# The last row of the last weight: loaded, multiplied, added and stored in two halves

## The chip, the cores and the metric

One core of a Trainium2 chip. The metric is device time in microseconds (us) of that core; lower is better. The **time** is the metric. The **span** is what the profile covers, from the first to the last recorded instruction. Each run reports both, the span to 0.1 us. Time minus span is called **the time outside the span**.

In the lines of the profile, PE is TensorE, which multiplies (PEld is its loading of weights), DVE is VectorE, ACT is ScalarE, POOL is GpSimd and SP is the sync engine; a q after the name marks the engine's sequencer, which also issues the transfers (DMA), so "the ACT queue" is ACT issuing a transfer. SBUF is the core's working memory, PSUM the memory, in banks, in which TensorE sums. A load has **landed** when the last of its writes to a semaphore, the counter that engines wait on, is recorded. The **tail** is what lies between the last landing of w4 and the end of the span.

## The reference, cut to what matters

The kernel decodes one token: an attention block over a cache of 65536 keys and values (4 heads of 128, bf16) and, in parallel, a small MLP; both outputs are added to the residual.

```
A = attention(xn, k_cache, v_cache, wq) @ wo            # o (4096) @ wo (4096 x 1024)
B = x1 + gelu(layernorm(x1) @ w3) @ w4                  # gh (3584) @ w4 (3584 x 1024)
out = x + A + B                                         # 1024 numbers, bf16
```

Everything that is read once per call comes from HBM, 170 MB, and w4 comes last.

## The kernel before: the parts the change touches

w4 is kept as 128 partitions by 28 rows of 1024 columns: row r on partition p is weight row 28p + r. It arrives in four loads; the last brings row 27 alone. One bank of PSUM collects the 1024 outputs as four strips of 256 columns, in partitions 0, 32, 64 and 96, which four column groups of TensorE fill side by side: the last row's four matmuls start within 10 ns of each other and take 270 ns each.

```python
w4_parts = [(0, 17), (17, 7), (24, 3), (27, 1)]          # (first row, rows): one load each, sync queue
OUT = S_ps[:, 0, 0:256]                                  # PSUM bank 0

def out_rows(items, reads, last=False):
    fns = []
    for lhs, rhs in items:                               # gh column r (128x1), w4 row r (128x1024)
        for jj in range(4):
            fns.append(lambda e, lhs=lhs, rhs=rhs, jj=jj: e.matmul(
                S_ps[32 * jj:32 * jj + 1, 0, 0:256], lhs, rhs[:, 256 * jj:256 * jj + 256],
                start=False, stop=last, tile_position=(0, 32 * jj), skip_group_check=True))
    _grp(q_pe, fns, reads=reads, writes=[b_OUT], partial=True)
...
resid_rows()          # residual into bank 1
wo_rows()             # attention output @ wo into bank 1, then moved to bank 0
for i, (r0, nr) in enumerate(w4_parts):
    out_rows([(gh_bf[:, r:r + 1], KV[:, 2, r * D:(r + 1) * D]) for r in range(r0, r0 + nr)],
             [b_W4[i], b_gh], last=(i == len(w4_parts) - 1))
_op(q_dve, lambda e: e.tensor_copy(orow[:, :], OUT), ...)                 # cast to bf16
ev_out = _dma(q_sp, chan("out"), lambda e: e.dma_start(out=..., in_=orow[0:97:32, :]), ...)
q_sp.wait_all([ev_out])
```

## Time and profile before

| | before |
|---|---|
| time, median | 400.6 us (400.57 to 400.77, 3 runs) |
| span of the profiled run | 399.08 us |
| bytes read | 169.87 MB, 426 GB/s over the span |
| last landing of w4 to the end of the span | 2.52 us |

The kernel is a stream of loads with a short tail: the packets of the loads fill 98.7% of the 16 DMA engines' span, and what the engines compute is hidden under the loads, except for what must follow the last landing. The prediction below shows the lines. Two more from the page's DMA part: the number of DMA packets, and the packets that carry instructions rather than data.

```profile
DMA packets 3759, 169.97 MB, mean 426 GB/s; under 512 B 548, under 2 KB 552, under 8 KB 808
...
q8 instruction: 5, 0.08, 0.1%
```

### The profile page before, as it was taken

To read this page: it belongs to the slowest core of one execution; us is meant where nothing else is said; L and a number is where in the kernel's file an instruction comes from. 1 tells how busy PE (TensorE), PEld (TensorE's weight loads), DVE (VectorE), ACT (ScalarE), POOL (GpSimd) and SP (SyncE) were. 2 spreads that over 40 slices of the span, in tenths; PEclk is the share of its full clock that TensorE was granted. 3 is DMA by queue.
4 is the path that set the end of the run, shared out by engine and by line. 5 is a ranking of instruction groups with operands and counts; after the bars stand their busy time and mean duration, and the time that the engine had idled before them with its cause. 6 is when DMAs were issued, how large, how long until landed. Compare 5 with 4: busy or idle time off the path is not lost.

```text
span 399.1 us, 3429 instructions
## 1 busy us (share of the span) xinstructions
PE 168.9 (42%) x1523; PEld 59.0 (15%) x1484; DVE 221.4 (55%) x260; ACT 23.9 (6%) x50; POOL 7.7 (2%) x31
## 2 busy tenths in 40 slices
PE   0034767338033713460357036413541362137394
PEld 0011334012001210110012001101120110012232
DVE  0024222994298549833984597269647952895201
ACT  1000000011001100110011002000100110011000
POOL 5000000000000000000000000000000000000000
PEclk9998568555655665575557555855585558555969
DMA  9999899999999999999999999999999999999995
GB/s 420 420 388 493 383 441 466 447 415 427 420 427 429 434 460 434 434 427 420 434 427 420 466 440 434 421 420 434 427 427 466 434 440 420 420 427 434 418 414 229
DMA packets 3759, 169.97 MB, mean 426 GB/s; under 512 B 548, under 2 KB 552, under 8 KB 808
## 3 DMA queue, kind: packets, MB, share of 16 engines
q1 hardware_dynamic: 3608, 169.87, 98.7%
q8 instruction: 5, 0.08, 0.1%
q10 hardware_dynamic: 144, 0.00, 0.0%
q14 instruction: 2, 0.02, 0.0%
HBM read 169.87 MB, written 0.00 MB: 426 GB/s over the span
## 4 chain that ended last, share of the span: by engine, by line
DMA 59%; DVE 25%; PE 12%; issue 1%; ACT 1%; SPq 1%; POOL 0%
DMA KV<-in_A_k_cache_dram 45%; DVE KV L460 18%; DMA KV<-in_B_w_dram 8%; DMA KV<-in_A_x_dram 6%; PE S_ps L411 3%; PE OT_ps L518 2%; DVE mrow L481 2%; PE M_ps L426 2%; PE S_ps L474 2%; PE S_ps L379 1%; ACT p_sb L496 1%; DVE Yall L395 1%; DVE pT_f L509 1%; DVE pT_f L419 1%; PE PT_ps L505 0%
## 5 line engine op out<-in xcount | busy, mean ns | idle before, releaser
L460 DVE STREAM_TRANSPOSE KV<-KV 128x4096 f32<-128x4096 f32 x32 | 140.3, 4422 | 44.3 <-DMA KV<-in_A_k_cache_dram 44.3
L474 PE MATMUL S_ps<-KV,Ycur 128*32 128x512 bf16 x512 | 60.7, 624 | 132.5 <-DVE KV L460 132.5
L518 PE MATMUL OT_ps<-KV,pT_f 128*32 128x512 bf16 x512 | 47.2, 511 | 4.0 <-issue 3.0
L474 PEld LDWEIGHTS S_ps<-KV,Ycur 128*32 128x32 bf16 x512 | 14.3, 126 | 160.0 <-DVE KV L460 142.4
L496 ACT ACTIVATE p_sb<-S_ps,brun 128x1024 bf16<-128x1024 f32 x16 | 17.8, 1114 | 276.6 <-DVE brun L494 176.1
L509 DVE STREAM_TRANSPOSE pT_f<-PT_ps 128x512 f32<-128x512 f32 x32 | 22.5, 702 | 14.0 <-PE PT_ps L505 14.0
L481 DVE TENSOR_REDUCE mrow<-S_ps 128x1 f32<-128x1024 f32 x16 | 19.3, 1205 | 11.3 <-PE S_ps L474 11.3
L484 PE MATMUL M_ps<-Rm,Lmat 128*128 128x16 bf16 x16 | 3.1, 194 | 38.0 <-DVE Rm L482 38.0
L529 DVE SCALAR_TENSOR_TENSOR O_acc<-O_acc,ff,OT_ps 128x512 f32<-128x512 f32 x12 | 9.0, 748 | 14.7 <-PE OT_ps L518 14.7
L518 PEld LDWEIGHTS OT_ps<-KV,pT_f 128*32 128x32 bf16 x512 | 13.1, 115 | 23.8 <-issue 16.4
L411 PE MATMUL S_ps<-KV 128*32 128x512 bf16 x88 | 12.1, 538 | 2.7 <-DVE KV L359 2.7
L339 DVE CAST KV<-KV 128x8 f32<-128x8 bf16 x1 | 0.2, 172 | 22.2 <-DMA KV<-in_A_x_dram 22.2
L578 PE MATMUL S_ps<-KV,o_bf 128*1 128x512 bf16 x64 | 9.9, 484 | 4.5 <-DMA KV<-in_A_wo_dram 4.5
L505 PE MATMUL PT_ps<-p_sb,permR 128*128 128x512 bf16 x16 | 9.7, 607 | 0.8
L426 PE MATMUL M_ps<-ident_f,pT_f 64*128 64x2 f32 (+2 forms) x32 | 7.9, 373 | 2.5 <-DVE pT_f L419 2.5
L484 PEld LDWEIGHTS M_ps<-Rm,Lmat 128*128 128x128 bf16 x16 | 1.7, 104 | 49.3 <-DVE Rm L482 49.3
L582 DVE COPY pT_f<-S_ps 1x512 f32<-1x512 f32 x1 | 0.7, 679 | 14.4 <-PE S_ps L578 14.4
L426 PEld LDWEIGHTS M_ps<-ident_f,pT_f 64*128 64x128 f32 (+2 forms) x32 | 7.7, 326 | 4.7 <-DVE pT_f L419 3.1
L419 DVE COPY pT_f<-S_ps 64x512 f32<-64x512 f32 (+1 forms) x3 | 2.1, 685 | 10.8 <-PE S_ps L411 10.8
L505 PEld LDWEIGHTS PT_ps<-p_sb,permR 128*128 128x128 bf16 x32 | 3.3, 102 | 27.5 <-ACT p_sb L496 14.7
L364 PE MATMUL M_ps<-KV 8*128 8x8 bf16 x1 | 0.2, 184 | 16.1 <-DVE Dmat_f L363 16.1
L642 POOL MEMSET pT_f<- 64x512 f32 x1 | 0.5, 520 | 312.4 <-PE OT_ps L518 312.4
(88 smaller groups left out, 90.2 us busy)
## 6 DMA issues: line engine op xcount, KB each, us to landing
KV<-in_B_w_dram SPq DMA_DIRECT2D x1, 7168.0 KB, 48.0
KV<-in_B_w_dram SPq DMA_DIRECT2D x1, 4352.0 KB, 27.4
KV<-in_B_w_dram SPq DMA_DIRECT2D x2, 2048.0 KB, 28.3
KV<-in_B_w_dram SPq DMA_DIRECT2D x1, 1792.0 KB, 31.3
KV<-in_B_w_dram SPq DMA_DIRECT2D x1, 768.0 KB, 32.7
KV<-in_B_w_dram SPq DMA_DIRECT2D x1, 256.0 KB, 32.9
KV<-in_A_k_cache_dram SPq DMA_DIRECT2D x8, 46.7
KV<-in_A_v_cache_dram SPq DMA_DIRECT2D x8, 28.1
```

The lines of the kernel that those rows point to most:

```text
L411: fns.append(lambda e, j=j, k=k, mv=mv: e.matmul(S_ps[32 * (k % 4):32 * (k % 4) + 32, bank + k // 4, :], vec[:, j:j + 1].broadcast_to([P, ...
L419: _op(q_dve, lambda e, b=b, nb=nb: e.tensor_copy(pT_f[0:32 * nb, b, :], S_ps[0:32 * nb, bank + b, :]), reads=[b_S[bank + b]], writes=[b_pT ...
L426: fns.append(lambda e, b=b, nb=nb, c=c: e.matmul(M_ps[:, c0 + 16 * b + c:c0 + 16 * b + 4 * nb:4], pT_f[0:32 * nb, b, c:512:4], ident_f[0:3 ...
L460: _op(q_dve, lambda e: e.transpose(out=KV32[:, s, o:o + 4096], in_=KV32[:, s, o:o + 4096]), reads=[b_KV[s][sub]], writes=[b_KV[s][sub]], l ...
L474: fns.append(lambda e, we=we, cm=cm, mv=mv: e.matmul(S_ps[32 * cm:32 * cm + 32, n % 4, :], Ycur[:, we, :, :].rearrange("p a g -> p (a g)") ...
L481: _op(q_dve, lambda e: e.reduce_max(mrow[:, k:k + 1], S_ps[:, 2 * k:2 * k + 2, :].rearrange("p b c -> p (b c)"), axis=AX.X), reads=b_S[2 * ...
L496: _op(q_act, lambda e: e.activation(p_sb[:, :, :].rearrange("p b c -> p (b c)"), S_ps[:, 2 * k:2 * k + 2, :].rearrange("p b c -> p (b c)") ...
L505: _op(q_pe, lambda e: e.matmul(PT_ps[:, :], permR[:, :], p_sb[:, n % 2, :], start=True, stop=True), reads=[b_p[n % 2], b_const], writes=[b ...
L509: _op(q_dve, lambda e: e.transpose(out=pT_f[:, n % 2, :], in_=PT_ps[:, :]), reads=[b_PT], writes=[b_pT[n % 2]], loop=True)
L518: fns.append(lambda e, q=q, q4=q4: e.matmul(OT_ps[32 * q4:32 * q4 + 32, g % 2, :], pT_bf[:, n % 2, q, :, 1], KV[:, s, 8192 * sub + 512 * q ...
L529: _op(q_dve, lambda e: e.scalar_tensor_tensor(out=O_acc[:, 0:512], in0=O_acc[:, 0:512], scalar=ff[:, k:k + 1], in1=OT_ps[:, k, :], op0=ALU ...
L578: _grp(q_pe, [lambda e, j=j, jj=jj: e.matmul(S_ps[32 * jj:32 * jj + 1, 1, :], o_bf[:, j:j + 1], KV[:, 0, j * D + 512 * jj:j * D + 512 * (j ...
```

## The change

The intent is a shorter tail. The last row arrives as two loads of 512 columns. Rows 0 to 23, the residual and wo are summed in bank 0 as before, but that sum is copied to SBUF ahead of time; rows 24 to 27 go into two other banks, one for each half of the columns. When a half has landed, its four matmuls have 128 columns, one add of 128 columns joins the bank with the copied sum and casts, and a store writes that half: the first from the ACT queue, the second from the sync queue. The second half's matmuls reuse the weights that the first half loaded. To make the halves contiguous, the columns of all strips are permuted (the residual and wo groups change addresses only). Cut to its core:

```diff
-w4_parts = [(0, 17), (17, 7), (24, 3), (27, 1)]
+w4_parts = [(0, 17 * D), (17 * D, 24 * D), (24 * D, 27 * D), (27 * D, 27 * D + 512), (27 * D + 512, 28 * D)]
...
+        def out_halves(r, halves, i, first=False, last=False):
+            def mm(e, hf, jj):
+                f = kept_matmul if halves == (1,) else ...          # ordinary matmul, fresh weights
+                return f(e, S_ps[32 * jj:32 * jj + 1, 2 + hf, 0:128], gh_bf[:, r:r + 1], w4_row(r, jj)[:, hf, :], (0, 32 * jj))
...
-        for i, (r0, nr) in enumerate(w4_parts):
-            out_rows(...)
-        _op(q_dve, lambda e: e.tensor_copy(orow[:, :], OUT), reads=[b_OUT], writes=[b_orow])
-        ev_out = _dma(q_sp, chan("out"), lambda e: e.dma_start(out=..., in_=orow[0:97:32, :]), reads=[b_orow])
-        q_sp.wait_all([ev_out])
+        for i in range(n_bulk):                                     # rows 0 to 23
+            out_rows(i)
+        _op(q_dve, lambda e: e.tensor_copy(ost, S_ps[:, 0, 0:256]), reads=[b_S[0]], writes=[b_ost])
+        for r in range(24, 27):
+            out_halves(r, (0, 1), 2, first=(r == 24))
+        ev_out = []
+        for hf, q_out in ((0, q_act), (1, q_sp)):
+            out_halves(27, (hf,), 3 + hf, last=True)
+            _op(q_dve, lambda e, hf=hf: e.tensor_tensor(out=orow[:, 128 * hf:128 * hf + 128],
+                in0=ost[:, 128 * hf:128 * hf + 128], in1=S_ps[:, 2 + hf, 0:128], op=ALU.add), ...)
+            ev_out.append(_dma(q_out, chan("out%d" % hf), lambda e, hf=hf: e.dma_start(out=..., in_=...), ...))
+        q_sp.wait_all(ev_out)
```

More of the change, by code (lines that the diff above doesn't have):

```diff
@@ L286, in bass_parallel_sum__gqa_block_cached__mixer_s_mlp__decode_kernel @@
         b_mrow = [_B(), _B()]; b_R = [_B(), _B()]; b_B = [_B(), _B()]; b_brun = [_B(), _B()]; b_dd = [_B(), _B()]; b_ff = [_B(), _B()]; b_lp = [_B(), _B()]
-        b_Oacc = _B(); b_L = _B(); b_cb = _B(); b_cbW = _B(); b_Mc = _B(); b_o = _B(); b_orow = _B()
+        b_Oacc = _B(); b_L = _B(); b_cb = _B(); b_cbW = _B(); b_Mc = _B(); b_o = _B(); b_orow = [_B(), _B()]
         def kv_load(s, ch, src, n, bufs=None):
@@ L550, in combine, with weights_of, keep_weights @@
             _op(q_dve, lambda e: e.tensor_copy(o_bf[32 * h:32 * h + 32, :], cb_o[0:32, :]), reads=[b_cb], writes=[b_o], partial=True)
-        w4_parts = [(0, 17), (17, 7), (24, 3), (27, 1)]
+        def weights_of(i):
+            return (i.tile_position, i.tile_size, str(i.ins[1].memref), i.ins[1].offset, str(i.ins[1].ap))
+        def keep_weights(i, name=""):
+            r = mybir.InstMatmult(name=name or i.name, engine=i.engine, ins=list(i.ins), outs=list(i.outs), debug=i.debug, start_tensor_calc=i.start_tensor_calc,
+                                  stop_tensor_calc=i.stop_tensor_calc, tile_size=i.tile_size, tile_position=i.tile_position,
+                                  bass_skip_group_check=i.bass_skip_group_check, ldweights=False)
+            return r
@@ new lines, in kept_matmul @@
+        def kept_matmul(e, out_, lhs, rhs, pos):
+            i = e.matmul(out_, lhs, rhs, start=False, stop=True, tile_position=pos, skip_group_check=True).ins
+            body = nc.m.functions[0].blocks[-1].instructions
+            at = max(k for k, j in enumerate(body) if j.name == i.name)
+            assert body[at].opcode == "Matmult" and any(j.opcode == "Matmult" and weights_of(j) == weights_of(i) for j in body[at - 6:at])
+            del body[at]
+            return e.add_instruction(keep_weights(i, "I-%d" % (1000000 + int(i.name[2:]))))
@@ L553, in bass_parallel_sum__gqa_block_cached__mixer_s_mlp__decode_kernel @@
+        w4_parts = [(0, 17 * D), (17 * D, 24 * D), (24 * D, 27 * D), (27 * D, 27 * D + 512), (27 * D + 512, 28 * D)]
         b_W4 = [_B() for _ in w4_parts]
         def w4_dma(i):
-            r0, nr = w4_parts[i]
-            _dma(q_sp, chan("w4%d" % i), lambda e: e.dma_start(out=KV[:, 2, r0 * D:(r0 + nr) * D], in_=rows_src(B_w4, r0, nr)), writes=[b_W4[i]])
-        OUT = S_ps[:, 0, 0:256]
-        b_OUT = b_S[0]
-        def out_rows(items, reads, last=False):
-            fns = []
-            for lhs, rhs in items:
-                for jj in range(4):
-                    fns.append(lambda e, lhs=lhs, rhs=rhs, jj=jj: e.matmul(
-                        S_ps[32 * jj:32 * jj + 1, 0, 0:256], lhs, rhs[:, 256 * jj:256 * jj + 256],
-                        start=False, stop=last, tile_position=(0, 32 * jj), skip_group_check=True))
-            _grp(q_pe, fns, reads=reads, writes=[b_OUT], partial=True)
+            c0, c1 = w4_parts[i]
+            _dma(q_sp, chan("w4%d" % i), lambda e: e.dma_start(out=KV[:, 2, c0:c1], in_=rows_src(B_w4, 0, KT_F)[:, c0:c1]), writes=[b_W4[i]])
@@ new lines, in bass_parallel_sum__gqa_block_cached__mixer_s_mlp__decode_kernel, with w4_row, out_rows @@
+        n_bulk = 2
+        b_half = [b_S[2], b_S[3]]
+        ost = pT_f[:, 1, 0:256]
+        b_ost = b_pT[1]
+        def w4_row(r, jj):
+            return KV[:, 2, r * D:(r + 1) * D].rearrange("p (h j n) -> p j h n", h=2, j=4)[:, jj, :, :]
+        def out_rows(i):
+            c0, c1 = w4_parts[i]
+            _grp(q_pe, [lambda e, r=r, jj=jj: e.matmul(
+                S_ps[32 * jj:32 * jj + 1, 0, 0:256].rearrange("p (h n) -> p h n", h=2), gh_bf[:, r:r + 1], w4_row(r, jj),
+                start=False, stop=(i == n_bulk - 1), tile_position=(0, 32 * jj), skip_group_check=True) for r in range(c0 // D, c1 // D) for jj in range(4)],
+                reads=[b_W4[i], b_gh], writes=[b_S[0]], partial=True)
@@ new lines, in out_halves @@
+        def out_halves(r, halves, i, first=False, last=False):
+            def mm(e, hf, jj):
+                f = kept_matmul if halves == (1,) else lambda e, *a: e.matmul(*a[:3], start=first, stop=last, tile_position=a[3], skip_group_check=True)
+                return f(e, S_ps[32 * jj:32 * jj + 1, 2 + hf, 0:128], gh_bf[:, r:r + 1], w4_row(r, jj)[:, hf, :], (0, 32 * jj))
+            _grp(q_pe, [lambda e, hf=hf, jj=jj: mm(e, hf, jj) for hf in halves for jj in range(4)],
+                 reads=[b_W4[i], b_gh], writes=[b_half[hf] for hf in halves], partial=not first)
@@ L571, in resid_rows @@
         def resid_rows():
+            idc = ident_f[:, :].rearrange("p (h j n) -> p j h n", h=2, j=2)
             _grp(q_pe, [lambda e, j=j, jj=jj: e.matmul(
-                S_ps[32 * jj:32 * jj + 1, 1, j:512:8], acc[:, j:j + 1], ident_f[:, 64 * jj:64 * jj + 64],
+                S_ps[32 * jj:32 * jj + 1, 1, :].rearrange("p (h n e) -> p h n e", h=2, e=8)[:, :, :, j], acc[:, j:j + 1], idc[:, jj, :, :],
                 start=(j == 0), stop=False, tile_position=(0, 32 * jj), skip_group_check=True) for j in range(KT_D) for jj in range(2)],
@@ L578, in wo_rows @@
             _grp(q_pe, [lambda e, j=j, jj=jj: e.matmul(
-                S_ps[32 * jj:32 * jj + 1, 1, :], o_bf[:, j:j + 1], KV[:, 0, j * D + 512 * jj:j * D + 512 * (jj + 1)],
+                S_ps[32 * jj:32 * jj + 1, 1, :].rearrange("p (h n) -> p h n", h=2), o_bf[:, j:j + 1],
+                KV[:, 0, j * D:(j + 1) * D].rearrange("p (h j n) -> p j h n", h=2, j=2)[:, jj, :, :],
                 start=False, stop=(j == 31), tile_position=(0, 32 * jj), skip_group_check=True) for j in range(32) for jj in range(2)],
@@ L583, in wo_rows @@
             _op(q_act, lambda e: e.activation(pT_f[32:33, 0, :], S_ps[32:33, 1, :], ACTF.Copy), reads=[b_S[1], b_pT[0]], writes=[b_pT[1]])
+            src = pT_f[0:64, 0, :].rearrange("p (h j n) -> p j h n", h=2, j=2)
             _grp(q_pe, [lambda e, jj=jj: e.matmul(
-                S_ps[32 * jj:32 * jj + 1, 0, 0:256], ident_f[0:64, 32 * (jj // 2):32 * (jj // 2) + 1], pT_f[0:64, 0, 256 * (jj % 2):256 * (jj % 2) + 256],
+                S_ps[32 * jj:32 * jj + 1, 0, 0:256].rearrange("p (h n) -> p h n", h=2), ident_f[0:64, 32 * (jj // 2):32 * (jj // 2) + 1], src[:, jj % 2, :, :],
                 start=True, stop=False, tile_position=(0, 32 * jj), skip_group_check=True) for jj in range(4)],
-                reads=[b_pT[0], b_pT[1], b_const], writes=[b_OUT])
+                reads=[b_pT[0], b_pT[1], b_const], writes=[b_S[0]])
         def loop_sync(h):
@@ L644, in bass_parallel_sum__gqa_block_cached__mixer_s_mlp__decode_kernel @@
         wo_rows()
-        for i, (r0, nr) in enumerate(w4_parts):
-            out_rows([(gh_bf[:, r:r + 1], KV[:, 2, r * D:(r + 1) * D]) for r in range(r0, r0 + nr)], [b_W4[i], b_gh], last=(i == len(w4_parts) - 1))
-        _op(q_dve, lambda e: e.tensor_copy(orow[:, :], OUT), reads=[b_OUT], writes=[b_orow])
-        ev_out = _dma(q_sp, chan("out"), lambda e: e.dma_start(out=out[0, 0, :].rearrange("(j n) -> j n", j=4), in_=orow[0:97:32, :]), reads=[b_orow])
-        q_sp.wait_all([ev_out])
+        for i in range(n_bulk):
[6 more added lines that the diff above has]
+            out_halves(27, (hf,), 3 + hf, last=True)
+            _op(q_dve, lambda e, hf=hf: e.tensor_tensor(out=orow[:, 128 * hf:128 * hf + 128], in0=ost[:, 128 * hf:128 * hf + 128], in1=S_ps[:, 2 + hf, 0:128], op=ALU.add),
+                reads=[b_ost, b_half[hf]], writes=[b_orow[hf]])
+            ev_out.append(_dma(q_out, chan("out%d" % hf), lambda e, hf=hf: e.dma_start(
+                out=out[0, 0, 512 * hf:512 * hf + 512].rearrange("(j n) -> j n", j=4), in_=orow[0:97:32, 128 * hf:128 * hf + 128]), reads=[b_orow[hf]]))
+        q_sp.wait_all(ev_out)
         code = nc.m.functions[0].blocks[0].instructions
@@ L706, in bass_parallel_sum__gqa_block_cached__mixer_s_mlp__decode_kernel @@
                 continue
-            key = (i.tile_position, i.tile_size, str(i.ins[1].memref), i.ins[1].offset, str(i.ins[1].ap))
+            key = weights_of(i)
             if key == prev and i.ins[1].dtype == BF and not i.sync_info:
-                code[k] = mybir.InstMatmult(name=i.name, engine=i.engine, ins=list(i.ins), outs=list(i.outs), debug=i.debug, start_tensor_calc=i.start_tensor_calc,
-                                            stop_tensor_calc=i.stop_tensor_calc, tile_size=i.tile_size, tile_position=i.tile_position,
-                                            bass_skip_group_check=i.bass_skip_group_check, ldweights=False)
+                code[k] = keep_weights(i)
                 n_ld += 1
```

## The prediction

> **What bounds the kernel now.** I read the page first, slices and chain. The DMA engines are at nine tenths or more in every slice but the last, in which the rate falls from 414 to 229 GB/s:
>
> ```profile
> DMA  9999899999999999999999999999999999999995
> GB/s 420 420 388 493 383 441 466 447 415 427 420 427 429 434 460 434 434 427 420 434 427 420 466 440 434 421 420 434 427 427 466 434 440 420 420 427 434 418 414 229
> ```
>
> So some 397 us of the 399.1 are one stream of loads, 169.87 MB that the change leaves alone. Only what follows the last landing can be shortened, or what delays it. The chain in order of time (start, length, what) shows that tail:
>
> ```profile
> 363.64 32.91 DMA KV<-in_B_w_dram
> 396.56 0.04 issue
> 396.60 0.31 PE S_ps L566 x4
> 396.91 0.02 issue
> 396.94 0.42 DVE orow L647
> ```
>
> The last row of w4 lands at 396.56; four matmuls, one cast to bf16 and a store follow. The timeline of the last microseconds (start, length, engine, line) gives the parts, and the waits at the end:
>
> ```profile
> 373.94 1.06 PE L572 MATMUL S_ps<-ident_f,acc 128*1 128x64 f32 x30
> 374.14 0.28 DVE L546 TENSOR_TENSOR cb_R<-M_ps,maskD 32x128 f32<-32x128 f32 x1 [1.15 <-PE M_ps L543]
> ...
> 391.37 2.03 PE L566 MATMUL S_ps<-KV,gh_bf 128*1 128x256 bf16 x68
> ...
> 394.09 0.93 PE L566 MATMUL S_ps<-KV,gh_bf 128*1 128x256 bf16 x28 [0.69 <-DMA KV<-in_B_w_dram]
> ...
> 395.95 0.50 PE L566 MATMUL S_ps<-KV,gh_bf 128*1 128x256 bf16 x12 [0.93 <-DMA KV<-in_B_w_dram]
> ...
> 396.60 0.28 PE L566 MATMUL S_ps<-KV,gh_bf 128*1 128x256 bf16 x4 [0.15 <-DMA KV<-in_B_w_dram]
> 396.94 0.42 DVE L647 CAST orow<-S_ps 128x256 bf16<-128x256 f32 x1 [6.78 <-PE S_ps L566]
> 397.39 0.63 SPq L648 DMA_DIRECT2D out_dram<-orow  x1
> ```
>
> From 396.56 to the end at 399.08 it is 2.52 us: 0.38 from the landing to the cast, 0.42 cast, 0.03, 0.63 issue of the store, 1.06 until the store has landed and the last wait is over. TensorE waits for DMA before each of its last three groups, so its work on them is hidden except for the last four matmuls. One thing more, from the table of stretches of half a microsecond:
>
> ```profile
> 395.00:395.50 0.50, 0.02 (x4) 0.00 (x0) 0.00 (x0) 0.00 (x0) 0.00 (x0) 1.00 0.31 119
> 395.50:396.00 0.50, 0.05 (x4) 0.05 (x8) 0.00 (x0) 0.00 (x0) 0.00 (x0) 1.00 0.15 57
> 396.00:396.50 0.50, 0.45 (x12) 0.14 (x12) 0.00 (x0) 0.00 (x0) 0.00 (x0) 1.00 0.01 4
> ```
>
> The last two columns are the share of 16 engines and GB/s. A third of the engines, or fewer, move the end of the stream, and the last data moved about half a microsecond before the landing is seen. In the trace's single DMA records 11 engines have reported the last row by 395.1, and five only between 396.0 and 396.56, each some 0.45 us after its last packet. The change does not touch why these five are late.
>
> [...] a 2048-byte packet takes 84 ns and follows the one before after 80, a 6144-byte one takes 238, so a packet of 1024 bytes should follow after about 80 - 1024*(238-84)/4096 = 41.5 ns, 1.5 ns more than half of 80. [...] Before, the store is four packets of 512 bytes (29 to 35 ns each); after, eight of 256. No packet of before shows what that costs in a store. [...] the 30 fp32 matmuls of 64 columns above take as much array time as 128 bf16 columns (fp32 at 256 columns takes two passes of about 215 ns each in the trace, bf16 about 109), and in two interleaved column groups, each with its own weight load, they advance (1.06 - 0.22)/15 = 0.056 us a pair. [...] The trace has 279 for such an operation with one operand in PSUM (the 0.28 line above); I use 0.28.
>
> **The change part by part.**
>
> Load of the last row: one 256 KB load of 2048-byte rows becomes two of 128 KB with 1024-byte rows. A late engine has 8 packets of 80 ns before. After, 16 of 41.5 = 664 instead of 640, and one more semaphore packet (9 ns long, the next starts about 6 later): the last landing comes **+0.03 us** later, the first half about 8 x 41.5 = 0.33 earlier than that, at about 396.26. The fifth issue on the sync queue costs about 0.43 us (four took 1.75), but at 364, 31 us before its data: 0.
>
> Rows 0 to 23 stay at 96 matmuls of 256 columns; the residual and wo rows keep count and size, only their addresses are permuted. Their PE work ends at 395.02 and is hidden. Then the new copy of the sum, PSUM to SBUF, 128x256: about the cast's 0.42, so done by 395.5 while VectorE is otherwise idle. 0.
>
> Rows 24 to 26: 12 matmuls of 256 columns become 24 of 128. Four column groups run side by side: before 2 x 0.109 + 0.272 + 0.01 = 0.50, as shown. After 5 x 0.056 + 0.22 = 0.50, over by 396.45. The first half's four matmuls can start at 396.30 (landing 396.26 + 0.04), finish at 396.53, and its add runs from 396.58 to 396.86. Hidden behind the second half, though closely.
>
> Second half: four matmuls of 128 columns, weights kept. [...] Leaving out the weight load I count as nothing: from the start of the last matmul to the dependent VectorE start it is 0.322 us here with a fresh load, and 0.309 in the attention's last product (same array time, weights loaded well ahead), so at most 0.01.
>
> Final VectorE operation: cast of 256 columns, 0.425, becomes an add of 128 columns, 0.28: **-0.145 us**. With the last landing at 396.59, TensorE starts at 396.63, ends at 396.86, and the second add can start at 396.91, 0.05 us after the first add has ended.
>
> Store: the first half goes on the ACT queue at about 396.9, the second on SP about 0.3 later. The issue time of 0.63 and the 1.06 after it I keep[...]. 0.
>
> Sum: 0.03 - 0.053 - 0.145 = **-0.17 us**. 400.60 - 0.17 = 400.43; I say **400.4 us**.
>
> **Rivals.** (a) *The first half stands in the way.* If the two landings come closer than 0.3 us, or the first add takes 0.35, the second add waits for VectorE; it gives back up to 0.28: 400.4 to 400.7. For it: the margin of 0.05. Against it: on one engine 8 packets of 1024 bytes need 0.33 and the same late engine ends both. (b) *The second store waits for the first*, or 256-byte writes take longer to be acknowledged. [...] the issues, 0.63 each and 0.3 apart, overlap. At the start the SP and ACT issues overlap for 0.27 and take 0.39 and 0.37, which speaks against; if the SP issue had to wait out the ACT issue, +0.3: 400.7. (c) *1024-byte packets cost more than the line through 2048 and 6144 says.* At 60 ns apiece the last landing is +0.3 and all gain is gone: 400.7. Against: even 16-byte packets are recorded at 9 ns. (d) *Instruction fetch or drift in the stream*: one 16 KB instruction packet near 394.3 took 1.08 us and competes with an engine; moved, it could shift the late engines by some tenths either way. TensorE cannot become the bound: it would have to lose the 0.9 us it waits before row 24.
>
> **Range and chances.** Three runs before spread over 0.20 us. Rivals a to c each cost about 0.3 and are each perhaps one in five; a second such term together is rare. So 400.1 to 400.8 should hold the median 8 times in 10. Two per cent is 8 us, and the whole tail after the last landing is 2.5, so neither faster nor slower by 2% is in reach of any step: 0.98 within, 0.01 each side.
>
> **What would show it.** Packets of the page up by about 150 (128 data, 16 and 4 semaphores, 4 of the store). In the chain: two landings about 0.33 apart, the last four matmuls at about 0.22, a VectorE add of 0.28 instead of 0.42, then a store of 0.63. From the last landing to the end 2.32 instead of 2.52. Rival a shows as a second add that waits for the first one and not for TensorE; b as an SP issue over 0.63 or more than 1.06 after it; c as halves more than 0.4 apart and 1024-byte packets well over 45 ns. The prediction is wrong if the change in time is not found after the last landing at all but in when the stream of loads ends: then a few tenths of drift hide the 0.17.

The sum still came to 0.03 - 0.053 - 0.145 = -0.17 us, but the working of the -0.053, for 128 matmul columns fewer, is cut, and so is the reason why a smaller store should keep its times, which was the author's estimate. Another estimate, from the trace of the kernel before, gives the same 0.053: four column groups of 256 bf16 columns advance by 0.109 us (L566), the 64-column fp32 records that the text takes for 128 bf16 columns by 0.056 (L572). For the add, 0.28 is the 279 ns of the TENSOR_TENSOR at L546, on 32 partitions by 128 columns of fp32. And "nine tenths or more in every slice but the last" overlooks the fifth slice, which shows 8.

## The result, and the profile after

| | before | changed |
|---|---|---|
| time, median (range) of 6 runs each | 400.59 (400.38 to 400.77) | 400.62 (400.37 to 400.83) |
| span of the profiled run | 399.08 | 398.86 |
| last landing of w4 to the end of the span | 2.52 | 2.34 |

Ratio 1.0001, 95% interval 0.9988 to 1.0013: the same time. (A ratio is the mean time of one kernel's fast runs over that of the other's fast runs of the same rounds, so not quite the ratio of the medians quoted.)

The span and the tail show the gain that the prediction added up; the time does not. The page's counts first:

```profile
DMA packets 3911, 169.97 MB, mean 426 GB/s; under 512 B 576, under 2 KB 832, under 8 KB 960
...
q8 instruction: 5, 0.08, 0.1%
```

There are 152 packets more, the 128 + 16 + 4 + 4 foreseen. The chain of waits (start, length, what) now ends so:

```profile
395.82 0.04 issue
395.87 0.61 PE S_ps L593 x28
396.48 0.03 issue
396.51 0.02 DVEq L73
396.53 0.04 issue
396.57 0.54 DVE orow L683 x2
```

The chain runs through the first half's add, because the record shows no idle time between the two adds; that does not mean that the second add waited for the first (see below). The timeline (start, length, engine, line) has the second half beside it:

```profile
393.97 0.94 PE L586 MATMUL S_ps<-KV,gh_bf 128*1 128x256 bf16 x28 [1.08 <-DMA KV<-in_B_w_dram]
394.96 0.42 DVE L677 COPY pT_f<-S_ps 128x256 f32<-128x256 f32 x1 [5.31 <-PE S_ps L586]
...
395.87 0.58 PE L593 MATMUL S_ps<-KV,gh_bf 128*1 128x128 bf16 x28 [0.96 <-DMA KV<-in_B_w_dram]
396.56 0.22 PE L562 MATMUL S_ps<-KV,gh_bf 128*1 128x128 bf16 x4
396.57 0.54 DVE L683 TENSOR_TENSOR orow<-pT_f,S_ps 128x128 bf16<-128x128 f32 x2 [1.19 <-PE S_ps L593]
396.89 1.09 ACTq L685 DMA_DIRECT2D out_dram<-orow  x1
397.14 0.62 SPq L685 DMA_DIRECT2D out_dram<-orow  x1
```

The copy at 394.96 is over long before it is needed. L593 holds rows 24 to 26 and the first half of row 27 (28 matmuls), L562 the second half. The two adds take 0.29 us each and overlap by 0.03. From the start of the last four matmuls to the end of the span it is 398.86 - 396.56 = 2.30 us; before it was 399.08 - 396.60 = 2.48. By the trace's semaphore records the halves landed at 396.18 and 396.52, and before the whole row landed at 396.56. One thing is new to the prediction: the issue of the store takes 1.09 us on ACT and 0.62 on the sync queue.

### The profile page after: what moved, and what is told of

Same layout as the page of the kernel before. It is cut to its first block, busy times and chain, and to the rows that moved or that the text cites. A ratio compares the mean times of both kernels' runs of the same rounds, so it can differ in the third digit from the quotient of the medians.

```text
span 398.9 us, 3478 instructions
## 1 busy us (share of the span) xinstructions
PE 176.9 (44%) x1555; PEld 58.9 (15%) x1496; DVE 221.8 (56%) x262; ACT 23.9 (6%) x50; POOL 7.6 (2%) x31
## 4 chain that ended last, share of the span: by engine, by line
DMA 58%; DVE 25%; PE 13%; issue 1%; ACT 1%; SPq 0%; POOL 0%; DVEq 0%
DMA KV<-in_A_k_cache_dram 44%; DVE KV L460 18%; DMA KV<-in_B_w_dram 8%; DMA KV<-in_A_x_dram 6%; PE S_ps L411 3%; PE OT_ps L518 2%; DVE mrow L481 2%; PE M_ps L426 2%; PE S_ps L474 2%; PE S_ps L379 2%; ACT p_sb L496 1%; DVE Yall L395 1%; DVE pT_f L509 1%; PE PT_ps L505 1%; DVE pT_f L419 1%
## 5 line engine op out<-in xcount | busy, mean ns | idle before, releaser
L505 PE MATMUL PT_ps<-p_sb,permR 128*128 128x512 bf16 x32 | 18.5, 579 | 0.8
L411 PE MATMUL S_ps<-KV 128*32 128x512 bf16 x88 | 12.5, 565 | 2.7 <-DVE KV L359 2.7
L379 PE MATMUL S_ps<-KV 128*32 128x512 bf16 x64 | 6.3, 577 | 1.4 <-DVE KV L359 1.4
```

The costliest lines, as they stand in the source:

```text
L379: fns.append(lambda e, j=j, b=b, jj=jj: e.matmul(S_ps[32 * jj:32 * jj + 32, b, :], xn_bf[:, j:j + 1].broadcast_to([P, 32]), KV[:, 0, j * H ...
L411: fns.append(lambda e, j=j, k=k, mv=mv: e.matmul(S_ps[32 * (k % 4):32 * (k % 4) + 32, bank + k // 4, :], vec[:, j:j + 1].broadcast_to([P, ...
L505: _op(q_pe, lambda e: e.matmul(PT_ps[:, :], permR[:, :], p_sb[:, n % 2, :], start=True, stop=True), reads=[b_p[n % 2], b_const], writes=[b ...
```

## The experiments

Two theories at the start, and more that the first runs forced. *A*: the tail is 0.18 us shorter and the end of the load stream drifts from run to run, so six runs do not show it. *B*: the change makes the stream itself end later and gives the gain back there. Twelve experiments were made, in three sets, of five rounds each (c4 three); two of them are repeats without an edit. All gave the right output. The third set ran on another chip than the first two. Each set has nine runs of the kernel before of its own, and those agree: 1.30, 1.28 and 1.29 us outside the span. The table is read from left to right: mean time, mean span and their difference over all runs, and, from the profiled run alone, the tail from the last landing of w4 to the end of the span. "ACT" counts the instructions that ACT's program has more than in the kernel before.

| kernel | ACT | runs | time, median | time, mean | span, mean | outside, mean (range) | tail |
|---|---|---|---|---|---|---|---|
| before (three sets) | 0 | 27 | 400.50 | 400.50 | 399.21 | 1.29 (1.21 to 1.39) | 2.52 |
| changed (first result) | +1 | 6 | 400.62 | 400.60 | 399.07 | 1.54 (1.47 to 1.64) | 2.34 |
| a1_again | +1 | 5 | 400.66 | 400.67 | 399.10 | 1.57 (1.51 to 1.65) | 2.34 |
| a2_split_load_only | 0 | 5 | 400.56 | 400.64 | 399.34 | 1.30 (1.22 to 1.39) | 2.60 |
| a3_one_queue | 0 | 5 | 400.54 | 400.61 | 399.36 | 1.25 (1.22 to 1.36) | 2.64 |
| a4_sum_ahead_only | 0 | 5 | 400.60 | 400.61 | 399.26 | 1.35 (1.23 to 1.40) | 2.63 |
| b1_one_store | 0 | 5 | 400.31 | 400.37 | 399.06 | 1.31 (1.21 to 1.40) | 2.35 |
| b2_queues_swapped | +1 | 5 | 400.74 | 400.76 | 399.22 | 1.54 (1.48 to 1.64) | 2.54 |
| b3_before_store_on_act | +1 | 5 | 400.63 | 400.66 | 399.16 | 1.50 (1.47 to 1.53) | 2.54 |
| b4_before_late_act | +2 | 5 | 400.84 | 400.89 | 399.28 | 1.61 (1.58 to 1.64) | 2.51 |
| c1_early_act | +2 | 5 | 400.89 | 400.88 | 399.24 | 1.64 (1.58 to 1.71) | 2.52 |
| c2_bulk_copy_on_act | +1 | 5 | 400.54 | 400.67 | 399.14 | 1.53 (1.46 to 1.64) | 2.40 |
| c3_one_store_again | 0 | 5 | 400.40 | 400.39 | 399.08 | 1.31 (1.24 to 1.40) | 2.35 |
| c4_more_fetches | 0 | 4 | 401.68 | 401.86 | 400.60 | 1.26 (1.20 to 1.30) | 2.52 |

Every interval of a ratio but that of c4 contains 1 (the intervals are about 0.13% wide to each side, 0.5 us), so single medians decide nothing here. What decides is the difference of the two columns, which is steady, and the tail. No run of a kernel with ACT at 0 has more than 1.40 us outside, none of the others less than 1.46.

### First set: the change again, and its parts alone

**a1_again**: the changed kernel, no edit.

> The changed kernel as it is, in more rounds. Theory A (the tail after the last landing is 0.18 us shorter, 2.34 instead of 2.52 us, and the end of the load stream only drifts from run to run): 400.4, that is 0.15 to 0.2 us under the kernel before in the mean, with single runs spread over 0.3 to 0.5 us. Theory B (the change itself makes the stream end later, by more packets, one more issue and five more semaphore writes, and so gives the 0.18 us back): no difference, 400.6.

The median was 400.66, ratio 1.0005 (0.9991 to 1.0018); the tail was 2.34 again. Over both sets the changed kernel's 11 spans have a mean of 399.08 us against 399.21 for the 27 of before: 0.13 us shorter, about twice its standard error of 0.06, in line with theory A. But the time outside the span is 1.55 us against 1.29. This is neither A nor B: the stream does not end later, and yet the time does not fall.

**a2_split_load_only**: the kernel before, with only the load split.

```diff
-w4_parts = [(0, 17), (17, 7), (24, 3), (27, 1)]
+w4_parts = [(0, 17 * D), (17 * D, 24 * D), (24 * D, 27 * D), (27 * D, 27 * D + 512), (27 * D + 512, 28 * D)]
 # the matmuls of row 27 wait for both halves
```

> The kernel before with only the load of the last row cut in two halves of 1024-byte rows; matmuls, cast and the one store wait for both and are as before. Theory A: the last landing 0.03 us later, so 400.63, not to be told from before. Theory B: the stream ends about 0.2 us later, so 400.8, and the tail after the landing stays at 2.52 us.

```profile
396.86 0.12 PEld L566 LDWEIGHTS S_ps<-KV,gh_bf 128*1 128x1 bf16 x4 [0.56 <-DMA KV<-in_B_w_dram]
396.89 0.28 PE L566 MATMUL S_ps<-KV,gh_bf 128*1 128x256 bf16 x4 [0.30 <-DMA KV<-in_B_w_dram]
397.22 0.42 DVE L647 CAST orow<-S_ps 128x256 bf16<-128x256 f32 x1 [8.08 <-PE S_ps L566]
```

The last half landed at 396.76 by the semaphore records, and the first matmul started 0.13 us later instead of 0.04: this group waits for two semaphores, and the later start is the tail's extra 0.08. The median of 400.56 is within 0.03 of before; theory B's 400.8 did not come. Its mean span is 0.13 over before, but one run of 399.8 makes nearly all of that.

**a3_one_queue**: the changed kernel, both stores from the sync queue.

```diff
-        for hf, q_out in ((0, q_act), (1, q_sp)):
+        for hf, q_out in ((0, q_sp), (1, q_sp)):
```

> The changed kernel with both stores issued from the sync queue. The second store can be issued only after the first one's 0.63 us of issue: it starts at about 397.5 instead of 397.14 on the trace's scale, so the tail is 0.37 us longer than in the changed kernel, 2.7 us. Theory A: 400.8, which is 0.2 us over the kernel before and 0.37 us over the changed one. Theory B: 401.0. If the median does not move at all, the tail does not set the time.

```profile
396.69 0.22 PE L562 MATMUL S_ps<-KV,gh_bf 128*1 128x128 bf16 x4
396.70 0.55 DVE L683 TENSOR_TENSOR orow<-pT_f,S_ps 128x128 bf16<-128x128 f32 x2 [1.18 <-PE S_ps L593]
397.01 1.19 SPq L685 DMA_DIRECT2D out_dram<-orow  x2
```

The two issues, back to back, end at 398.20; in the changed kernel the sync queue's issue was over at 397.76 (397.14 + 0.62). The tail grew to 2.64, 0.30 over the changed kernel (0.37 was expected), and the mean span by 0.28. Yet theory A's 400.8 did not come; the mean time is 400.61 beside 400.63: what the span lost, the time outside gained, 1.25 instead of 1.55. That was the clue that the difference outside the span hangs on the ACT queue or on ACT.

**a4_sum_ahead_only**: the halves undone, the sum ahead kept.

```diff
-... (27 * D, 27 * D + 512), (27 * D + 512, 28 * D)]
+... (27 * D, 28 * D)]
-  (two banks, two adds of 128 columns, two stores)
+  _op(q_dve, lambda e: e.tensor_tensor(out=orow[:, :], in0=ost, in1=S_ps[:, 2, 0:256], op=ALU.add), ...)
+  (one store, sync queue)
```

> The changed kernel with its halves undone: rows 0 to 23 still summed ahead into SBUF, but row 27 comes as one load, its four matmuls have 256 columns, one add of 256 columns in place of the cast, one store. The add[...] costs what the cast costs, so theory A: tail 2.52 us as before, 400.6. Theory B: also 400.6, for the load is as before; with a2 the two parts of the change stand alone.

```profile
396.66 0.28 PE L592 MATMUL S_ps<-KV,gh_bf 128*1 128x256 bf16 x4 [0.15 <-DMA KV<-in_B_w_dram]
397.07 0.42 DVE L680 TENSOR_TENSOR orow<-pT_f,S_ps 128x256 bf16<-128x256 f32 x1 [1.51 <-PE S_ps L592]
397.52 0.67 SPq L683 DMA_DIRECT2D out_dram<-orow  x1
```

The add of 256 columns takes the cast's 0.42, as expected. The tail is 0.11 longer than before all the same: the add starts 0.13 us after the matmuls end (396.66 + 0.28) where the cast started 0.06 after (396.60 + 0.28 to 396.94), because it waits for two semaphores, TensorE's and VectorE's own, the first through an instruction of its own (the "DVEq L73" of the chains, 0.02 us, with 0.03 of issue before it and 0.04 after); the rest is in the issue of the store, which is now eight pieces of 256 bytes: 0.67 us instead of 0.63, and 1.06 after it as before. In the changed kernel only the first half's add has this double wait, where it is hidden. So the sum ahead alone gains nothing; the halves are what shortens the tail.

### Second set: what adds time outside the span

Theory D: a store issued from ACT near the end adds 0.25 us outside the span. Theory E: the halves do.

**b1_one_store**: the changed kernel with one store for both halves.

```diff
-            ev_out.append(_dma(q_out, chan("out%d" % hf), ...))        # in the loop over the halves
+        ev_out.append(_dma(q_sp, chan("out0"), lambda e: e.dma_start(  # after it
+            out=out[0, 0, :].rearrange("(h j n) -> j h n", h=2, j=4), in_=orow[0:97:32, :].rearrange("p (h n) -> p h n", h=2)), reads=b_orow))
```

> The changed kernel with both halves of the load, products and adds, but one store on the sync queue after the second add, as in the kernel before. So far the span of the changed kernel is 0.15 us shorter than before in the mean (399.08 and 399.24), as the sum said, while the time outside the span (time minus span) went from 1.30 to 1.55 us. Theory D (a store issued from ACT at the end adds about 0.25 us outside the span): span 0.13 us shorter than before, outside 1.30 as before, so the time is 0.13 us under the kernel before, about 400.4. Theory E (the time outside grows with the halves, not with the ACT queue): outside 1.55, time 400.65.

```profile
396.75 0.23 PE L562 MATMUL S_ps<-KV,gh_bf 128*1 128x128 bf16 x4
396.76 0.55 DVE L683 TENSOR_TENSOR orow<-pT_f,S_ps 128x128 bf16<-128x128 f32 x2 [1.17 <-PE S_ps L593]
397.34 0.67 SPq L685 DMA_DIRECT2D out_dram<-orow  x1
```

One issue of 0.67 us after the second add, and nothing on ACT. The tail is 2.35, as in the changed kernel; outside it is 1.31. Both parts of theory D's expectation came, theory E is out.

**b2_queues_swapped**: `((0, q_sp), (1, q_act))`.

> The changed kernel with the queues swapped: first half's store from the sync queue, second half's from ACT. Theory D: the time outside the span is 1.55 us again or more, as the ACT store now comes 0.26 us later; the span as in the changed kernel within 0.05 us if an ACT store lands as soon after its issue starts as one from the sync queue (1.25 and 1.27 us to the first packet in the trace). If the longer ACT issue (1.09 against 0.63 us) counts for the landing, the span grows by up to 0.45 us.

Outside 1.54, as D said. The tail of 2.54 is not a clean reading of the queues: TensorE's granted clock had fallen in this profile, to 0.79 and then 0.50 (the third number from the right in the table of stretches is PEclk),

```profile
396.00:396.50 0.50, 0.45 (x28) 0.44 (x28) 0.00 (x0) 0.00 (x0) 0.00 (x0) 0.79 0.03 10
396.50:397.00 0.50, 0.50 (x16) 0.00 (x0) 0.10 (x1) 0.00 (x0) 0.00 (x0) 0.50 0.00 0
```

so the matmuls and the first add came late. In the single records the second add started 0.21 us after the first and 0.09 after its own matmuls, where the changed kernel has 0.26 and 0.04. That may be the prediction's rival in which the first half stands in the way, or the slow clock alone; one profile does not tell.

**b3_before_store_on_act**: the kernel before, its store issued from ACT.

```diff
-        ev_out = _dma(q_sp, chan("out"), ...)
+        ev_out = _dma(q_act, chan("out"), ...)
```

> The kernel before with nothing changed but its one store, issued from ACT in place of the sync queue. Theory D: span as before within 0.05 us, time outside the span 1.55 in place of 1.30, so the time is 0.25 us over the kernel before, 400.8. Theory E, or a theory that it takes two queues at once: outside 1.30, time 400.55.

```profile
397.25 1.08 ACTq L648 DMA_DIRECT2D out_dram<-orow  x1
```

Outside 1.50, and the tail 2.54, 0.02 from before: the longer issue on ACT did not delay the landing, but moving the store to ACT cost 0.2 us outside the span. Two queues or two halves are not needed for it.

**b4_before_late_act**: the kernel before, with two idle copies on ACT after the cast and the store still on the sync queue.

```diff
+        for t in range(2):
+            _op(q_act, lambda e, t=t: e.activation(cb_R[:, 64 * t:64 * t + 64], orow[:, 64 * t:64 * t + 64], ACTF.Copy), ...)
```

> The kernel before with two small copies on ACT after the final cast, into a buffer nobody reads, so that ACT is busy until about 398 as in the changed kernel, but issues no store. If it is ACT's late end that costs outside the span: outside 1.55, time 400.8. Theory D in the narrow sense (the store itself, not ACT's late end): outside 1.30, time 400.55 as before.

```profile
397.54 0.62 SPq L648 DMA_DIRECT2D out_dram<-orow  x1
397.55 0.54 ACT L650 ACTIVATE cb_R<-orow 128x64 f32<-128x64 bf16 x2 [6.71 <-DVE orow L647]
```

The copies run beside the store's issue and the tail is 2.51, but outside it is 1.61. So it is not the store: theory D in its narrow sense falls. It could be that ACT ends late, or that it has more instructions.

### Third set: late, or more?

**c1_early_act**: the same two copies, before the attention loop.

```diff
+        for t in range(2):                      # placed before the loop, about 70 us
+            _op(q_act, lambda e, t=t: e.activation(cb_R[:, 64 * t:64 * t + 64], ident_f[:, 64 * t:64 * t + 64], ACTF.Copy), ...)
```

> The kernel before with the same two small ACT copies as in the late-ACT run, but before the attention loop, at about 60 us. Theory L (it is ACT's being busy in the last microseconds that adds time outside the span): outside 1.29 us as before, time 400.5. Theory C (it is the count of ACT's instructions): outside 1.55 to 1.6, time 400.8.

```profile
70.57 0.53 ACT L454 ACTIVATE cb_R<-ident_f 128x64 f32<-128x64 f32 x2
86.02 1.11 ACT L498 ACTIVATE p_sb<-S_ps,brun 128x1024 bf16<-128x1024 f32 x1 [14.93 <-DVE brun L493]
```

They are done at 71 us, 15 us before ACT's next work, and hold up nothing in the span: its mean is 399.24. Outside it is 1.64 us, as with the late copies. Lateness is out; the count fits. It goes with ACT's count here, not with any engine's: the sync engine has two recorded instructions more in a3 than before, and GpSimd 520 more in c4 below, and these have 1.25 and 1.26 us outside.

**c2_bulk_copy_on_act**: the one-store version with the copy of rows 0 to 23 on ACT instead of VectorE.

> The one-store version with the hidden copy of rows 0 to 23 made by ACT instead of VectorE: ACT is busy to about 395.6, some 1.2 us before TensorE's and VectorE's own last work and 3.5 us before the end. The span should be as in the one-store version, 399.06, or 0.05 less. Theory L with a threshold of being the last of TensorE, VectorE and ACT to finish: outside 1.30 us, time 400.35. If any ACT work after the attention, however early, is enough: outside 1.55, time 400.6.

The mean span is the one-store version's within 0.08 (the profile's tail of 2.40 instead of 2.35 goes with last four matmuls of 0.27 us instead of 0.22, as in b2 at a granted clock of 0.50). Outside it is 1.53: one instruction more on ACT. This expectation was put in terms of how early ACT finishes; it got the answer "however early", which c1 explains better.

**c3_one_store_again**: no edit to b1.

> The one-store version again, to know whether it beats both kernels: span 0.15 us shorter than before and 1.30 us outside give 400.35 to 400.4, against 400.52 for the kernel before and 400.63 for the changed one. If its first five runs were luck: 400.5 or more.

Median 400.40, ratio 0.9998 (0.9984 to 1.0011). The ten runs of the one-store version have a mean of 400.38 us, against 400.50 for the 27 of before and 400.63 for the 11 of the changed kernel. It is the best of the three by its mean, by 0.12 and 0.25 us; each set's interval still contains 1, so against the kernel before it is likely rather than proven.

**c4_more_fetches**: the kernel before with 520 idle memsets on GpSimd. This one asks why a few engines always end the stream late.

```diff
+        for t in range(520):                    # before the loop, nobody waits for them
+            q_pool.op(lambda e, t=t: e.memset(pad_t[:].bitcast(mybir.dt.uint8)[:, t:t + 1], 0), tick=False)
```

> The kernel before with 520 one-column memsets on GpSimd after its set-up work, into an unused pad; nobody waits for them. They are 520 more instructions[...]. So far every trace has 5 such packets on the instruction queue and 5 of the 16 engines reporting the last row about a microsecond after the other 11. Theory F (each packet makes the engine that carries it late for good):[...] if an engine gets two, one that is two microseconds late and a time up to 1 us longer. If the lateness has nothing to do with instruction packets: 5 late engines, time 400.5.

```profile
q8 instruction: 5, 0.08, 0.1%
q14 instruction: 6, 0.05, 0.0%
```

The instruction packets of 16 KB stayed five (16384 bytes each); four more of 8 KB (8192 bytes) came on another queue, which had 2 before and 6 here. The memsets ran in groups of 128 with 1.8 to 1.9 us of idle time between them, in which GpSimd waited for nothing that the profile shows; nobody waited for GpSimd.

```profile
63.95 3.70 POOL L454 MEMSET pad<- 128x1 uint8 x128 [1.89 <-issue]
69.45 3.70 POOL L454 MEMSET pad<- 128x1 uint8 x128 [1.81 <-issue]
```

Instruction packets delayed the load stream here. In every trace, each one between 40 and 390 us is followed within 0.04 us by one load packet that takes 0.35 to 0.66 us longer than the median of its size; in the 13 other traces no other load packet of 14 KB or more is over 0.2 us longer after the first 3 us. In c4 eight engines reported the last row after 396.4 (five in the kernel before after 396.0), the first engine was 0.8 us later too, and the mean span grew by 1.4 us. But the profiled run, 2.6 us longer, is not clean: between 105.7 and 111.4 us 26 more load packets were up to 1.6 us longer, for a reason that the record does not show. The other three runs have a mean span of 400.23, 1.0 us over before, which is what theory F expected at most. That each late engine is one that carried such a packet is not settled, as the records do not name engines.

## Why the prediction was right or wrong

The median of 400.62 us lies within 400.1 to 400.8, and within 2%. That is no support for the mechanism, as the kernel before, at 400.59, lies in that range too; the range held because it allowed for no gain at all. The 0.17 us that it foresaw is seen in the tail of both profiles and in the mean span, and is missing in the time, so one step was wrong.

- **Tail**: 2.32 us from the last landing foreseen, 2.34 measured twice (2.52 before). Right.
- **Load**: halves 0.33 us apart foreseen, 0.34 measured (396.18 and 396.52). A packet of 1024 bytes is recorded at 46 ns; rival c (60 ns apiece) did not happen. a2 bears it out to the accuracy of its runs.
- **TensorE**: 0.22 for the last four matmuls foreseen and measured; a matmul took 0.216 us instead of 0.270, so the 0.053 came as foreseen, and rows 24 to 26 stayed hidden.
- **VectorE**: 0.28 foreseen, 0.29 measured (286 and 287 ns; the prediction's 279 is a reading of another operation). The first add started at 396.57, right where it was foreseen at 396.58, and would have been about 0.07 us earlier, by a4's measure, without its double wait. The second did not wait for the first in the changed kernel's profile: it started 0.04 us after its matmuls. Rival a was seen, if anywhere, in b2.
- **The second store held up by the first** (rival b): the sync issue took 0.62 us and the span ended 1.09 us after it by the single records, against 1.06 before. The store's packets took 18 ns each at 256 bytes, 29 to 35 at 512 before. No.
- **The store at 0 is the step that failed**: "Store: the first half goes on the ACT queue [...] The issue time of 0.63 and the 1.06 after it I keep [...] 0." In the span it is about 0, though the issue took 1.09 us on ACT. In the metric, which runs beyond the span, it cost 0.26 us (1.55 against 1.29), more than the 0.17 gained. b3 shows it for the store alone, b4, c1 and c2 show that a copy on ACT, late or early, does it without a store, and b1 that the gain stays when the store leaves ACT. So the prediction was wrong to look at the store's issue and landing alone; what it left out is a cost of one more instruction on ACT that no part of the span shows.
- **Drift**: the prediction took the time to be the span plus a constant and named drift in the end of the load stream as what could hide the gain. Drift there is (spans of the changed kernel from 398.9 to 399.4), but over 11 runs the gain shows in the span's mean, and what hid it was the other term.

What stays open: where the time outside the span lies. By the semaphore records the end of the program after the span is the same length to 5 ns, 1.43 us, in twelve of the fourteen traces, with none, one or two instructions more on ACT; only b3 (1.52) and c4 (1.47) differ. So the records after the span do not show it, and of b3's 0.2 us up to 0.09 may be something else. This end alone is longer than the 1.25 to 1.35 us outside the span of the kernels with ACT at 0, so the time is not simply the span and this end. And whether it is the count itself or something that goes with it is open: only one and two instructions more were tried, and the second added less than the first (about 0.1 us after about 0.25).

## What to carry to other kernels

When a change is worth tenths of a microsecond, read the span and the metric side by side over many runs: a gain in the one can be paid back in the part that no trace shows (here 0.17 us foreseen and 0.26 paid). Before spreading the last stores over queues, measure what the second queue costs by itself; here two halves of compute feeding one store kept the gain of the span, and the store on ACT spent it. The tail after the last load was shortened here by smaller last pieces (2.52 to 2.34 us), and an operation in it that waited for two semaphores started 0.07 (a4, VectorE) to 0.09 us (a2, TensorE) later than with one: let each wait for one where you can.
